# Attention in blocks and a feed-forward layer on one core: a new order for the first tile, its transpositions in single sum banks, and spare products

## The chip, the core and the metric

The kernel runs on one core of a Trainium2 chip. The core has TensorE (PE in the rows: matrix products into the sum banks, with PEld for its weight loads), VectorE (DVE), ScalarE (ACT), GpSimd (POOL) and SyncE (SP), which issues the transfers. The engines run side by side, each through its own instructions in order, and wait for each other by semaphores. Sums of TensorE stand in eight banks of 128 x 512 numbers. The metric is the device time of one execution in microseconds (us).

## The reference

For 8 batches, 8 heads, 576 positions and 64 features per head the kernel computes attention inside blocks of 64 positions, and then a layer with a residual over the 512 features of all heads:

```
scores = (q @ k.T) / sqrt(64)              # per block of 64 x 64
attn   = exp(scores - max); attn /= (sum(attn) + 1e-9)
x      = attn @ v                          # heads side by side: (8, 576, 512)
xn     = (x - mean) / sqrt(var + 1e-6) * g
out    = x + relu(xn @ w1) @ w2            # w1: 512 x 2048, w2: 2048 x 512
```

All arrays are 32-bit; the weights reach the kernel as 64-bit words and are turned into 32-bit numbers on the chip.

## The kernel before

The 4608 positions are cut into 18 pairs of 256 and 9 tiles of two pairs. For a pair, `attention` goes through thirteen steps: load q and k (L186), scores (L206), the maximum and the load of v (L213, L216), subtraction and exponential (L219, L223), the transposition of the probabilities `pt` (in the first two tiles by TensorE, L231, with copies by ScalarE), the products with v (L271; in the first tile with the row sums beside them, L275), x (L286), statistics (L304), `xg` (x less its mean, times g, L309), and the transposition of `xg` into `xt` (L321). `xt` is kept as a rounded high part `xth` (L324) and a low part `xtl`, which TensorE makes by adding the high part times minus one (`minus`) to the same sum bank (L328, L331).

`ffn` then takes 16 hidden blocks f: an up (12 products, L369), the high part `hh` and low part `hl` of its positive part (L377 on ScalarE, L378 on VectorE), and a down (six products for a pair, L389) into the pair's two sum banks `y`. In the first tile blocks 0 to 5 are done for each pair by itself (256 columns), the other ten for both (512 columns).

The weights come in 17 units (two half units, then 15 whole ones of 1.05 MB): fetched by SP (L104), absolute value on ScalarE (L112), rounding on VectorE (three operations, L119 to L123), the sign (L129), the high part by ScalarE (L133), and the low part `wl`, for the first four units by TensorE through the sum banks of pair 1 (L144 to L146), for the others by VectorE (L148). Three buffers hold fetched units, one the absolute values.

The sum banks: one buffer `s` of two banks, through which scores, `pt`, attention outputs and `xt` of every pair of the first two tiles pass in turn; two banks `h`; four banks `y`, two for each pair of a tile.

What stands where is written by hand: `START` is a string of letters, and each letter plays one step of one stream: a, b the attention of the first tile's pairs, A, B of the second tile's, E of the third's first pair; w the weights; u and 1, v and 2, y and 3 the products and the rectified parts of the first tile. `STEADY` and `LAST` order the other tiles. Each engine gets its instructions in that order, the SP queue too.

Of the kernel before, what the change touches and what calls it, by code (L numbers as in the profile page):

```python
# [13 lines left out]
AF = mybir.ActivationFunctionType  # L14
# [3 lines left out]
P = 128  # L18
# [5 lines left out]
NPAIR = T // PAIR  # L24
NTILE = NPAIR // 2
# [6 lines left out]

START = "aawwwwaawwwwwwawbwawwawbwbabwwaawaaawwbwwuA1wbbu1uwuwuAuB1Awubu1u1Awbwuu1bbbbuwvwAvw22AwAAvvvvB2EwA2wvv2vABvy2w3yBvwAww3vAyAwwywwyw3yA3BwyBwByByByBw3wB3wyByBww3yyBwwyEw3wywyy33yy3"
STEADY = "ABu1Au1AuAu1AuAu1AuABuAu1AEu1AuAu1AuAu1AuAu1BuBu1BuBu1BuBu1BuBEuBBu1BBu1BuBBu1Buu1uu1"
LAST = "u1u1uu1uu1uu1uu1uu1uu1uu1uu1uu1uu1uu1uu1uu1uu1u1"

SINGLE = 6

BY_PE = 4

ROOM = (3, 11)

# [9 lines left out]
def chunk_attention_ffn(ctx: ExitStack, tc: tile.TileContext, qkv, g, w, out):  # L54
# [15 lines left out]
    ident = const.tile([P, P], F32, name="ident")  # L70
    make_identity(nc, ident)
    minus = const.tile([P, P], F32R, name="minus")
    nc.scalar.activation(minus, ident, AF.Copy, scale=-1.0)
    ones = const.tile([P, 2], F32, name="ones")
    nc.gpsimd.memset(ones, 1.0)
    mhalf = const.tile([P, 2], F32, name="mhalf")
# [74 lines left out]
    def convert_w():  # L151
# [18 lines left out]
        split_w(units - 1)  # L170
        yield

    ys, taken = {}, set()

    def sums(pair):
# [5 lines left out]
    def attention(pair, xt_cols, xs, by_pe, den_by_pe):  # L181
# [10 lines left out]
        def banks():  # L192
            return ps_a.tile([P, 2, DM], F32, name="s")

        def rows(bank):
            return bank.rearrange("p (a d) -> p a d", d=D)

        s2 = banks()
        s = [rows(s2[:, h2, :]) for h2 in range(2)]
# [26 lines left out]

        pt_sb = work.tile([P, groups, 2, D], F32, name="pt_sb", tag="work")
        if by_pe:
            pt = banks().rearrange("p j (a t) -> p j a t", a=HP)
            for a in range(groups):  # L230
                nc.tensor.transpose(out=pt[:, a // HP, a % HP, :], in_=p_sb[:, a, :, :], identity=ident)  # L231
            for j in range(2):
                nc.scalar.copy(
                    pt_sb[:, j * HP : (j + 1) * HP], pt[:, j].rearrange("p a (c t) -> p a c t", c=2)
                )
            yield
        else:
            for h2 in range(2):
                for j in range(2):
                    for c in range(2):  # L240
                        for i in range(2):
                            nc.vector.transpose(  # L242
                                out=pt_sb[quad(2 * h2 + j), :, c, quad(i)], in_=p_sb[quad(2 * c + i), :, h2, quad(j)]
                            )
                    yield
# [67 lines left out]

        xth, xtl = xt_cols()
        if by_pe:
            xt = banks()
            for j in range(2):
                js = slice(j * P, (j + 1) * P)
                for k in range(NK):
                    ks = slice(k * P, (k + 1) * P)  # L320
                    nc.tensor.matmul(  # L321
                        xt[:, j, ks], lhsT=xg[:, j, ks], rhs=ident, is_transpose=True, start=k == 0, stop=k == NK - 1
                    )
                nc.scalar.copy(xth[:, :, js], xt[:, j, :].rearrange("p (k t) -> p k t", k=NK))  # L324
                yield
            for j in range(2):
                js = slice(j * P, (j + 1) * P)
                nc.tensor.matmul(  # L328
                    xt[:, j, :], lhsT=minus, rhs=xth[:, :, js], start=False, stop=True, skip_group_check=True
                )  # L330
                nc.scalar.copy(xtl[:, :, js], xt[:, j, :].rearrange("p (k t) -> p k t", k=NK))  # L331
                if j == 0:
                    yield
        else:
            xt = work.tile([P, 2 * NK, P], F32, name="xt", tag="work")
            xg = xg.rearrange("p j (k t) -> p (j k) t", k=NK)
            for j in range(4):
                for i in range(4):
                    nc.vector.transpose(out=xt[quad(j), :, quad(i)], in_=xg[quad(i), :, quad(j)])  # L339
                yield  # L340
            for j in range(2):
                js = slice(j * P, (j + 1) * P)
                xt_j = xt[:, j * NK : (j + 1) * NK, :]
                nc.scalar.copy(xth[:, :, js], xt_j)  # L344
                nc.gpsimd.tensor_tensor(out=xtl[:, :, js], in0=xt_j, in1=xth[:, :, js].bitcast(F32), op=ALU.subtract)  # L345
# [7 lines left out]
    def ffn(pairs, xt, xs, f0, f1, room=()):  # L353

        nt = len(pairs) * PAIR
        slots = DM // nt
        hs, held = {}, []
        tail = pairs[-1] == NPAIR - 1

        def up(f):  # L360
            assert 2 * f in converted and all(pair in xs for pair in pairs)
            h = ps_h.tile([P, nt], F32, name="h")
            xth, xtl = xt()
            m = 0
            for k in range(NK):
                ks = slice(k * P, (k + 1) * P)
                wh, wl = (x[:, ks] for x in weights(f))
                for wx, x in ((wh, xth), (wh, xtl), (wl, xth)):
                    nc.tensor.matmul(h, lhsT=wx, rhs=x[:, k, :], start=m == 0, stop=m == 3 * NK - 1)  # L369
                    m += 1  # L370
            hs[f] = h

        def split(f):
            if slots == 1 or not held:
                held[:] = [hp_.tile([P, slots, nt], F32R, name=f"h{i}") for i in "hl"]
            h, (hh, hl) = hs[f], (x[:, f % slots, :] for x in held)
            nc.scalar.activation(hh, h, AF.Relu)  # L377
            nc.vector.scalar_tensor_tensor(  # L378
                out=hl, in0=h, scalar=0.0, in1=hh.bitcast(F32), op0=ALU.max, op1=ALU.subtract
            )  # L380
            hs[f] = hh, hl

        def down(f, j):
            assert 2 * f + 1 in converted
            taken.add(pairs[j // 2])
            hh, hl = (x[:, j * P : (j + 1) * P] for x in hs[f])
            wh, wl = (x[:, DM:] for x in weights(f))
            for m, (hx, wx) in enumerate(((hh, wh), (hh, wl), (hl, wh))):
                nc.tensor.matmul(  # L389
                    sums(pairs[j // 2])[j % 2], lhsT=hx, rhs=wx,  # L390
                    start=f == 0 and m == 0, stop=f == NF - 1 and m == 2,
                )

        def finish(j):
            pair, jj = pairs[j // 2], j % 2
            x, rstd = xs[pair]
            nc.vector.scalar_tensor_tensor(  # L397
                out=x[:, jj, :], in0=sums(pair)[jj], scalar=rstd[:, jj : jj + 1], in1=x[:, jj, :],
                op0=ALU.mult, op1=ALU.add,
            )  # L400
            row = pair * PAIR + jj * P
            nc.sync.dma_start(out[row : row + P, :], x[:, jj, :])

        count = 2 * len(pairs)
        done = []

        def products():
            ups = iter(range(f0, f1))
            for f in range(f0, f1):
                for _ in range((f not in room) + (f == f0 or f - 1 in room or tail and f == NF - 3)):  # L410
                    i = next(ups, None)
                    if i is not None:
                        up(i)
                        yield
                if tail and f >= NF - 2:
                    continue
                for j in range(count):
                    down(f, j)
                done.append(f)
                yield  # L420
            if tail:
                for j in range(count):
                    for f in range(NF - 2, NF):
                        down(f, j)
                done.append(NF - 1)
                yield

        def rectified():
            for f in range(f0, f1):
                assert f < f0 + 2 or f - 2 in done  # L430
                split(f)
                yield
            if f1 == NF:
                assert NF - 1 in done
                for j in range(count):
                    finish(j)
                yield

        return products(), rectified()
# [3 lines left out]
    def play(order, streams):  # L443
        for c in order:
            next(streams[c])
# [3 lines left out]
    class Tokens:  # L449
# [18 lines left out]
    now = {  # L468
        "a": tiles[0].attention(0, True, True), "b": tiles[0].attention(1, True, True),
        "A": tiles[1].attention(0, True), "B": tiles[1].attention(1, True),  # L470
        "E": tiles[2].attention(0), "w": convert_w(),
    }
    now.update(zip("u1", tiles[0].ffn(0, 1, 0, SINGLE)))
    now.update(zip("v2", tiles[0].ffn(1, 1, 0, SINGLE)))
    now.update(zip("y3", tiles[0].ffn(0, 2, SINGLE, NF)))
    with tc.manual_schedule():
        play(START, now)
        for t in range(1, NTILE):
            now.update(zip("u1", tiles[t].ffn(0, 2, room=ROOM if t + 1 < NTILE else ())))
            if t + 1 < NTILE:  # L480
                now.update(A=now.pop("E"), B=tiles[t + 1].attention(1))
            now["E"] = tiles[t + 2].attention(0) if t + 2 < NTILE else iter("  ")
            play(STEADY if t + 1 < NTILE else LAST, now)
# [33 lines left out]
```

## Time and profile before

| | |
|---|---|
| median of 3 runs | 882.14 us (881.94 to 883.23) |
| profiled execution | 884.8 us, span 883.0 us |
| TensorE busy | 856.3 us, 97% of the span |
| VectorE, ScalarE, GpSimd busy | 538.3, 173.6, 50.6 us |
| loads and stores | 55.67 MB moved, mean 63 GB/s |

A busy time is the time in which an engine has at least one instruction running; start and duration of an instruction are those of the hardware profiler. The chain that ended last leads from the end back to what released each step. The granted clock of TensorE (PEclk) is 1.00 at 2.4 GHz and 0.50 at 1.2 GHz.

### The profile page before, as it was taken

The page shows a single profiled execution, that of the slowest core. Times are in us where ns is not written, and L with a number is a line of the kernel's source. Part 1 is how long each engine was busy: PE and PEld are TensorE (multiplying, and loading weights), DVE is VectorE, ACT ScalarE, POOL GpSimd, SP SyncE. Part 2 cuts the span into 40 slices and gives each one's busy share as a digit, 9 for nine tenths or more (in the row PEclk, how much of TensorE's full clock was granted, in tenths as well). Part 3 has the DMA queues.
Part 4 walks back from the last instruction along what each step waited for, and adds up shares of the span by engine and source line. Part 5 has one row for each costly group of instructions (what it writes and reads, how often), then busy time and mean ns, then how long its engine had stood idle before and what let it go on. Part 6 is the DMA issues. An engine that isn't in the chain of part 4 may idle for free.

```text
span 883.0 us, 13918 instructions
## 1 busy us (share of the span) xinstructions
PE 856.3 (97%) x6050; PEld 706.4 (80%) x6050; DVE 538.3 (61%) x963; ACT 173.6 (20%) x262; POOL 50.6 (6%) x54
## 2 busy tenths in 40 slices
PE   4699999999999999999999999999999999999998
PEld 3378788888888888888888888888888888888886
DVE  5988885657575666567656766666566657661112
ACT  4543541111111211021112120212120111111110
POOL 0000000010100110010101010101010101010000
PEclk9799999999999999999999999999999999999999
DMA  7554241310032003200320032003200210010001
GB/s 298 206 201 168 95 144 49 104 39 1 1 120 72 1 1 119 73 1 1 119 73 1 1 120 73 1 1 120 73 1 1 79 66 0 1 48 1 1 1 48
DMA packets 18205, 55.67 MB, mean 63 GB/s; under 512 B 2017, under 2 KB 2017, under 8 KB 16225
## 3 DMA queue, kind: packets, MB, share of 16 engines
q1 hardware_dynamic: 18000, 54.53, 17.4%
q8 instruction: 47, 0.77, 0.4%
q10 hardware_dynamic: 144, 0.26, 0.1%
q14 instruction: 14, 0.11, 0.0%
HBM read 45.35 MB, written 9.44 MB: 62 GB/s over the span
## 4 chain that ended last, share of the span: by engine, by line
PE 97%; DVE 1%; issue 1%; ACT 1%; DMA 1%; SPq 0%
PE y L389 45%; PE h L369 45%; PE s L206 2%; PE h L271 2%; PE s L231 1%; DMA k_t<-qkv 1%; PE y L144 1%; PE s L271 1%; PE s L321 0%; PE s L328 0%; ACT xtl L331 0%; ACT xth L324 0%; PE y L275 0%; DVE raw L123 0%; DVE top L213 0%
## 5 line engine op out<-in xcount | busy, mean ns | idle before, releaser
L369 PE MATMUL h<-xth,wp 128*128 128x512 f32 (+1 forms) x1200 | 379.3, 382 | 0.0
L389 PE MATMUL y<-wp,hh 128*128 128x512 f32 x1152 | 358.1, 392 | 0.0
L378 DVE SCALAR_TENSOR_TENSOR hl<-h,hh 128x512 fp32r<-128x512 f32 (+1 forms) x150 | 100.4, 669 | 285.5 <-ACT hh L377 285.0
L369 PEld LDWEIGHTS h<-xth,wp 128*128 128x128 f32 x1200 | 224.0, 189 | 43.5
L389 PEld LDWEIGHTS y<-wp,hh 128*128 128x128 f32 x1152 | 214.8, 188 | 44.7 <-ACT hh L377 0.2
L369 PE MATMUL h<-xtl,wp 128*128 128x512 f32 (+1 forms) x600 | 228.9, 381 | 0.0
L389 PE MATMUL y<-wp,hl 128*128 128x512 f32 x576 | 224.9, 390 | 0.0
L377 ACT ACTIVATE hh<-h 128x512 fp32r<-128x512 f32 (+1 forms) x150 | 87.1, 580 | 575.8 <-PE h L369 556.3
L369 PEld LDWEIGHTS h<-xtl,wp 128*128 128x128 f32 x600 | 113.3, 189 | 21.9
L389 PEld LDWEIGHTS y<-wp,hl 128*128 128x128 f32 x576 | 108.4, 188 | 23.2 <-DVE hl L378 0.4
L339 DVE STREAM_TRANSPOSE xt<-xg 32x256 f32<-32x256 f32 x224 | 97.7, 436 | 3.7
L242 DVE STREAM_TRANSPOSE pt_sb<-p_sb 32x256 f32<-32x256 f32 x224 | 97.6, 436 | 3.1
L345 POOL TENSOR_TENSOR xtl<-xt,xth 128x512 fp32r<-128x512 f32 x28 | 35.6, 1292 | 609.4 <-ACT xth L344 609.4
L397 DVE SCALAR_TENSOR_TENSOR x<-y,rstd,x 128x512 f32<-128x512 f32 x36 | 25.3, 750 | 18.4 <-PE y L389 18.4
L206 PE MATMUL s<-k_t,q_t 64*64 64x64 f32 x1152 | 21.3, 224 | 7.9 <-DMA k_t<-qkv 6.8
L213 DVE TENSOR_REDUCE top<-s 128x16 f32<-128x1024 f32 x18 | 21.9, 1216 | 9.6 <-PE s L206 9.6
L223 ACT ACTIVATE p_sb<-p_sb 128x1024 f32<-128x1024 f32 x18 | 19.1, 1061 | 44.0 <-DVE p_sb L219 44.0
L206 PEld LDWEIGHTS s<-k_t,q_t 64*64 64x64 f32 x1152 | 19.4, 140 | 9.4 <-issue 9.2
L294 DVE TENSOR_TENSOR x<-h,rden 128x512 f32<-128x512 f32 x28 | 18.0, 686 | 12.1 <-PE h L271 12.1
L309 DVE SCALAR_TENSOR_TENSOR xg<-x,mv,g_sb 128x512 f32<-128x512 f32 x36 | 25.3, 743 | 0.0
L304 DVE BATCH_NORM_STATS2 stats<-x 128x6 f32<-128x512 f32 x36 | 24.3, 675 | 0.3
L112 ACT ACTIVATE wf<-raw 128x1024 f32<-128x1024 f32 (+1 forms) x17 | 18.7, 1100 | 21.7 <-DMA raw<-w 13.1
(47 smaller groups left out, 306.5 us busy)
## 6 DMA issues: line engine op xcount, KB each, us to landing
raw<-w SPq DMA_DIRECT2D x15, 1024.0 KB, 4.8
q_t<-qkv SPq DMA_DIRECT2D x18, 512.0 KB, 4.6
k_t<-qkv SPq DMA_DIRECT2D x18, 512.0 KB, 5.5
v_t<-qkv SPq DMA_DIRECT2D x36, 256.0 KB, 4.9
out<-x SPq DMA_DIRECT2D x36, 256.0 KB, 2.1
raw<-w SPq DMA_DIRECT2D x2, 512.0 KB, 6.7
g_sb<-g ACTq DMA_DIRECT2D x1, 256.0 KB, 4.8
```

The source lines that it names most:

```text
L206: nc.tensor.matmul(s[h2][c * D : (c + 1) * D, j * HP + a, :], lhsT=q_t[r, a, cs], rhs=k_t[r, a, cs], start=True, stop=True,)
L242: nc.vector.transpose(out=pt_sb[quad(2 * h2 + j), :, c, quad(i)], in_=p_sb[quad(2 * c + i), :, h2, quad(j)])
L271: nc.tensor.matmul(rows(o[h2])[cs, ja, :], lhsT=lhsT, rhs=v_t[j][r, a, c, :], start=True, stop=True)
L304: nc.vector.bn_stats(out=stats, in_=x[:, j, :])
L309: nc.vector.scalar_tensor_tensor(out=xg[:, j, :], in0=x[:, j, :], scalar=mv[:, j, 0:1], in1=g_sb, op0=ALU.subtract, op1=ALU.mult)
L339: nc.vector.transpose(out=xt[quad(j), :, quad(i)], in_=xg[quad(i), :, quad(j)])
L345: nc.gpsimd.tensor_tensor(out=xtl[:, :, js], in0=xt_j, in1=xth[:, :, js].bitcast(F32), op=ALU.subtract)
L369: nc.tensor.matmul(h, lhsT=wx, rhs=x[:, k, :], start=m == 0, stop=m == 3 * NK - 1)
L377: nc.scalar.activation(hh, h, AF.Relu)
L378: nc.vector.scalar_tensor_tensor(out=hl, in0=h, scalar=0.0, in1=hh.bitcast(F32), op0=ALU.max, op1=ALU.subtract)
L389: nc.tensor.matmul(sums(pairs[j // 2])[j % 2], lhsT=hx, rhs=wx, start=f == 0 and m == 0, stop=f == NF - 1 and m == 2,)
L397: nc.vector.scalar_tensor_tensor(out=x[:, jj, :], in0=sums(pair)[jj], scalar=rstd[:, jj : jj + 1], in1=x[:, jj, :], op0=ALU.mult, op1=ALU.add,
```

## The change

Three things change. First, in the first tile `pt` and `xt` of a pair no longer take the two-bank buffer `s` but the pair's own two sum banks (`halves`), each half a bank for itself; `taken` only marks them in use while the order is recorded. Second, a stream `keep_warm`, letter k, issues eight products of `minus` with itself into the first sum bank; nobody reads them. The new order plays it four times: once ahead of everything, and three times in a row between the low part of the second half unit and the scores of pair 1. Third, `START` is new. `minus` is now made at the head of the recorded order.

```diff
-START = "aawwwwaawwwwwwawbwawwawbwbabwwaawaaawwbwwuA1wbbu1uwuwuAuB1Awubu1u1Awbwuu1bbbbuwvwAvw22AwAAvvvvB2EwA2wvv2vABvy2w3yBvwAww3vAyAwwywwyw3yA3BwyBwByByByBw3wB3wyByBww3yyBwwyEw3wywyy33yy3"
+START = "wkwwawwwwwwbwwawwkkkbaawawwbbwaabawaaawAbwbaauubbAw11bbAbbuwAuuwBAuAAv1uw1vA2uwuBw2w1wvwvv2uAw1uvAyuwvw2v3wyBywBvw23EvwwwAy2wAwywy3AAwwwyv3BwwyBBByByBwB3vB3Bywwyyw3wBywww3ywy3wyy3yy3E"
...
+WARM = 8
...
-    nc.scalar.activation(minus, ident, AF.Copy, scale=-1.0)
...
+    def keep_warm():
+        while True:
+            assert 0 not in taken
+            for i in range(WARM):
+                nc.tensor.matmul(sums(0)[0][:, :P], lhsT=minus, rhs=minus, start=True, stop=True)
+            yield
...
+        def halves():
+            if den_by_pe:
+                assert pair not in taken
+                return sums(pair)
+            both = banks()
+            return [both[:, j, :] for j in range(2)]
...
-            pt = banks().rearrange("p j (a t) -> p j a t", a=HP)
+            pt = halves()
             for a in range(groups):
-                nc.tensor.transpose(out=pt[:, a // HP, a % HP, :], in_=p_sb[:, a, :, :], identity=ident)
+                cs = slice(a % HP * P, (a % HP + 1) * P)
+                nc.tensor.transpose(out=pt[a // HP][:, cs], in_=p_sb[:, a, :, :], identity=ident)
...
-            xt = banks()
+            xt = halves()
+            if den_by_pe:
+                taken.add(pair)
...
-        "E": tiles[2].attention(0), "w": convert_w(),
+        "E": tiles[2].attention(0), "w": convert_w(), "k": keep_warm(),
...
     with tc.manual_schedule():
+        nc.scalar.activation(minus, ident, AF.Copy, scale=-1.0)
         play(START, now)
```

In the SP queue q and k of pair 0 stood first (L186), and then four fetches of weights (L104). Now the two half units and unit 2 are fetched first, then q and k of pair 0, unit 3, q and k of pair 1, unit 4 and v of pair 0.

VectorE, at the start of the program. `top` and `p_sb` belong to the attention, `wf` and `raw` to the weights. Before:

```order
L213 TENSOR_REDUCE top<-s 128x16
L219 TENSOR_TENSOR p_sb<-s,top 128x2x8x64
L119 TENSOR_SCALAR wf<-wf 128x512
L120 TENSOR_SCALAR wf<-wf 128x512
L123 SCALAR_TENSOR_TENSOR raw<-raw,wf 128x512
L129 SCALAR_TENSOR_TENSOR raw<-raw 128x512
```

and now, from the second half unit on (the first stands ahead of it in the same four rows):

```order
L120 TENSOR_SCALAR wf<-wf 128x512
L121 TENSOR_SCALAR wf<-wf 128x512
L124 SCALAR_TENSOR_TENSOR raw<-raw,wf 128x512
L130 SCALAR_TENSOR_TENSOR raw<-raw 128x512
L120 TENSOR_SCALAR wf<-wf 128x1024
L121 TENSOR_SCALAR wf<-wf 128x1024
L124 SCALAR_TENSOR_TENSOR raw<-raw,wf 128x1024
L130 SCALAR_TENSOR_TENSOR raw<-raw 128x1024
L230 TENSOR_REDUCE top<-s 128x16
L236 TENSOR_TENSOR p_sb<-s,top 128x2x8x64
```

Both half units and the first whole unit stand ahead of the first maximum, where none stood before.

VectorE, from the row sums of pair 0 (`den`) to its `xg`. Before:

```order
L281 TENSOR_SCALAR den<-y 128x8 x2
L282 RECIPROCAL rden<-den 128x16
L286 TENSOR_TENSOR x<-s,rden 128x2x8x64
L129 SCALAR_TENSOR_TENSOR raw<-raw 128x1024
L213 TENSOR_REDUCE top<-s 128x16
L304 BN_STATS stats<-x 128x6
L305 BN_AGGR mv<-stats 128x2
...
L219 TENSOR_TENSOR p_sb<-s,top 128x2x8x64
L119 TENSOR_SCALAR wf<-wf 128x1024
L120 TENSOR_SCALAR wf<-wf 128x1024
L123 SCALAR_TENSOR_TENSOR raw<-raw,wf 128x1024
L309 SCALAR_TENSOR_TENSOR xg<-x,mv,g_sb 128x512 x2
```

and now:

```order
L299 TENSOR_SCALAR den<-y 128x8 x2
L300 RECIPROCAL rden<-den 128x16
L304 TENSOR_TENSOR x<-s,rden 128x2x8x64
L322 BN_STATS stats<-x 128x6
L323 BN_AGGR mv<-stats 128x2
...
L327 SCALAR_TENSOR_TENSOR xg<-x,mv,g_sb 128x512 x2
L130 SCALAR_TENSOR_TENSOR raw<-raw 128x1024
```

The sign of a unit, the maximum and subtraction of pair 1 and a unit's rounding no longer stand between x and `xg`; the pair 1 steps have moved ahead of the row sums.

TensorE, at the start of the program, `y<-raw,ident` and `y<-wp,minus` being the low part of a half unit. Before:

```order
L206 MATMUL s<-k_t,q_t 64x64 x32
L144 MATMUL y<-raw,ident 128x512
L145 MATMUL y<-wp,minus 128x512
L231 MATMUL s<-ident,p_sb 128x128 x8
L144 MATMUL y<-raw,ident 128x512
```

and now:

```order
L179 MATMUL y<-minus 128x128 x8
L145 MATMUL y<-raw,ident 128x512
L146 MATMUL y<-wp,minus 128x512
L223 MATMUL s<-k_t,q_t 64x64 x32
L145 MATMUL y<-raw,ident 128x512
L146 MATMUL y<-wp,minus 128x512
L179 MATMUL y<-minus 128x128 x24
L223 MATMUL s<-k_t,q_t 64x64 x32
L249 MATMUL y<-ident,p_sb 128x128 x8
```

The spare products stand first and ahead of the second scores, the scores of both pairs ahead of the first transpositions, and these write `y` instead of `s`.

## Rows read from the trace of the kernel before

**Rows 1.** Stretches: length; busy (count) of PE, PEld, DVE, ACT, POOL; PEclk, DMA, GB/s

```profile
0.00:42.00 42.00, 21.78 (x301) 14.06 (x301) 30.47 (x41) 21.26 (x28) 1.98 (x9) 0.88 0.67 244
70.00:860.00 790.00, 789.33 (x5357) 654.61 (x5357) 478.73 (x881) 136.28 (x212) 47.04 (x44) 1.00 0.14 49
```

**Rows 2.** Waits of TensorE, 0 to 70 us: line, releaser, us, times, longest

```profile
PE s L321 <- DVE xg L309: 4.3, 1, 4.3
```

**Rows 3.** Timeline of VectorE: start, duration, line, operation

```profile
8.84 1.23 DVE L213 TENSOR_REDUCE top<-s 128x16 f32<-128x1024 f32 x1 [8.84 <-PE s L206]
...
11.24 0.42 DVE L119 TENSOR_SCALAR wf<-wf 128x512 f32<-128x512 f32 x1
...
13.62 0.43 DVE L119 TENSOR_SCALAR wf<-wf 128x512 f32<-128x512 f32 x1
...
23.05 0.23 DVE L281 TENSOR_SCALAR den<-y 128x8 f32<-128x8 f32 x2
...
24.75 1.22 DVE L129 SCALAR_TENSOR_TENSOR raw<-raw 128x1024 uint32<-128x1024 uint32 x1
...
27.47 0.68 DVE L304 BATCH_NORM_STATS2 stats<-x 128x6 f32<-128x512 f32 x1
...
29.09 1.19 DVE L219 TENSOR_TENSOR p_sb<-s,top 128x1024 f32<-128x1024 f32 x1
...
30.19 0.68 DVE L119 TENSOR_SCALAR wf<-wf 128x1024 f32<-128x1024 f32 x1
...
32.78 1.41 DVE L309 SCALAR_TENSOR_TENSOR xg<-x,mv,g_sb 128x512 f32<-128x512 f32 x2
...
34.11 1.22 DVE L129 SCALAR_TENSOR_TENSOR raw<-raw 128x1024 uint32<-128x1024 uint32 x1
...
81.32 0.39 DVE L378 SCALAR_TENSOR_TENSOR hl<-h,hh 128x256 fp32r<-128x256 f32 x1
```

**Rows 4.** Stretches around the fall and the rise of the granted clock (PEclk)

```profile
32.00:33.00 1.00, 0.00 (x0) 0.00 (x0) 1.00 (x2) 0.10 (x1) 0.00 (x0) 0.61 1.12 475
...
45.00:46.00 1.00, 1.00 (x52) 1.00 (x49) 0.75 (x2) 1.00 (x2) 0.00 (x0) 0.57 0.86 344
```

**Rows 5.** Chain that ended last, 0 to 72 us: start, us, what

```profile
6.80 1.99 PE s L206 x64
...
40.27 1.97 PE s L231 x8
...
42.24 2.56 PE h L369 x12
...
53.16 1.09 PE s L206 x64
...
57.26 1.43 PE h L369 x12
...
58.69 1.39 PE y L389 x6
...
67.30 2.56 PE y L389 x6
...
71.30 0.77 PE s L231 x7
```

**Rows 6.** Stretches from the start, for the data moved (last column GB/s)

```profile
0.00:5.35 5.35, 0.00 (x0) 0.00 (x0) 0.00 (x0) 1.28 (x1) 0.77 (x8) 1.00 0.66 216
0.00:6.67 6.67, 0.00 (x0) 0.00 (x0) 0.00 (x0) 1.28 (x1) 0.77 (x8) 1.00 0.73 254
0.00:11.60 11.60, 1.99 (x64) 1.83 (x64) 2.72 (x3) 2.39 (x4) 0.77 (x8) 1.00 0.85 324
```

**Rows 7.** Timeline of ScalarE

```profile
7.95 0.67 ACT L112 ACTIVATE wf<-raw 128x512 f32<-128x512 f32 x1 [5.50 <-DMA raw<-w]
...
11.36 1.06 ACT L223 ACTIVATE p_sb<-p_sb 128x1024 f32<-128x1024 f32 x1 [2.54 <-DVE p_sb L219]
```

**Rows 8.** Waits of VectorE, 47.3 to 141.4 us

```profile
DVE hl L378 <- ACT hh L377: 9.5, 9, 1.9
```

More of the change, by code (lines that the diff above doesn't have):

```diff
@@ L228, in attention @@
         if by_pe:
-            pt = banks().rearrange("p j (a t) -> p j a t", a=HP)
+            pt = halves()
             for a in range(groups):
-                nc.tensor.transpose(out=pt[:, a // HP, a % HP, :], in_=p_sb[:, a, :, :], identity=ident)
+                cs = slice(a % HP * P, (a % HP + 1) * P)
+                nc.tensor.transpose(out=pt[a // HP][:, cs], in_=p_sb[:, a, :, :], identity=ident)
             for j in range(2):
                 nc.scalar.copy(
-                    pt_sb[:, j * HP : (j + 1) * HP], pt[:, j].rearrange("p a (c t) -> p a c t", c=2)
+                    pt_sb[:, j * HP : (j + 1) * HP], pt[j].rearrange("p (a c t) -> p a c t", a=HP, c=2)
                 )
@@ L321, in attention @@
                     nc.tensor.matmul(
-                        xt[:, j, ks], lhsT=xg[:, j, ks], rhs=ident, is_transpose=True, start=k == 0, stop=k == NK - 1
+                        xt[j][:, ks], lhsT=xg[:, j, ks], rhs=ident, is_transpose=True, start=k == 0, stop=k == NK - 1
                     )
-                nc.scalar.copy(xth[:, :, js], xt[:, j, :].rearrange("p (k t) -> p k t", k=NK))
+                nc.scalar.copy(xth[:, :, js], xt[j].rearrange("p (k t) -> p k t", k=NK))
                 yield
@@ L328, in attention @@
                 nc.tensor.matmul(
-                    xt[:, j, :], lhsT=minus, rhs=xth[:, :, js], start=False, stop=True, skip_group_check=True
+                    xt[j], lhsT=minus, rhs=xth[:, :, js], start=False, stop=True, skip_group_check=True
                 )
-                nc.scalar.copy(xtl[:, :, js], xt[:, j, :].rearrange("p (k t) -> p k t", k=NK))
+                nc.scalar.copy(xtl[:, :, js], xt[j].rearrange("p (k t) -> p k t", k=NK))
                 if j == 0:
                     yield
+            if den_by_pe:
+                taken.remove(pair)
         else:
@@ L357, in ffn @@
         hs, held = {}, []
-        tail = pairs[-1] == NPAIR - 1
+        tail = pairs[-1] == 2 * NTILE - 1
         def up(f):
```

## The prediction

> **What bounds the kernel now.** I read the busy times of long stretches first. From 70 to 860 us TensorE is busy for 789.33 of 790 us at full clock, so nothing there can be gained or moved; from 0 to 42 us it is busy for only 21.78 [rows 1]. The change rewrites the order of the first tile alone, so the whole question lies in the first 70 us.
>
> Second, the waits of TensorE: 4.3 us for `xg`, a VectorE result, is the longest after the first keys, for which it stands until 6.80 us [rows 2, 5]. Third, therefore, VectorE's own timeline: it stands idle until the scores arrive at 8.84 us and then runs almost without a gap, turn by turn on weights and attention [rows 3]. Up to about 40 us TensorE waits for VectorE and, behind it, for the order of the loads.
>
> Fourth, the clock. It falls in the slice 32 to 33 us (0.61), inside TensorE's 4.3 us wait for `xg`, and rises in 45 to 46 us (0.57) [rows 2, 4]. At the low level 12 up products take 2.56 us instead of 1.43, and 6 down products 2.56 instead of 1.39 [rows 5]. The first 64 score products took 1.99 us against 1.09 later [rows 5], so the start ran at the low level too, although the slices there print 1.00.
>
> **The landmark for the sum.** At 69.86 us (67.30 + 2.56) the kernel before has finished all six hidden blocks of pair 0; from there it runs full [rows 5]. I look for the time at which the new order has done a known part of the same work and count the difference in warm durations. The landmark of the new order is the end of pair 2's eight probability transpositions (p of `A`). By then it has done all that the old one has done at 69.86, except three ups (blocks 3, 4, 5) and four downs (2 to 5), and it has done eight transpositions more, which the old one starts only at 71.30 us. The difference is 3 × 1.43 + 4 × 1.39 − 0.87 = 8.98 us (0.87 from 0.77 for the seven transpositions that the row shows) [rows 5].
>
> **When the first weights land.** In the new SP queue both half units of weights (0.52 MB each) and unit 2 (1.05 MB) stand ahead of the first queries and keys. The table g (0.26 MB) goes on another queue beside them. Before, the first keys ended 1.31 MB of queued data and were there just ahead of the scores at 6.80, about 6.67 us, when 254 × 6.67 = 1.69 MB had moved [rows 5, 6]: data land 0.38 MB behind their place. The first half unit now ends 0.78 MB, so it lands when 1.16 MB have moved, at 5.35 us (216 × 5.35) [rows 6]. The keys now end 3.41 MB and land at 3.79 MB, 11.6 us (324 × 11.6 = 3.76) [rows 6]: 4.9 us later than before. ScalarE's absolute value takes 0.67 us [rows 7]; VectorE starts at about 6.0 instead of 8.84. Bounds: with no lag at all 0.9 us earlier, with twice the lag 0.9 us later; I keep the middle, which is the measured lag.
>
> **VectorE's chain to the landmark.** Its queue is in order, so I add what stands in it, start to start [rows 3]: a half unit of weights 2.38; a full unit 2.59 to round (30.19 to 32.78) and 1.22 for the sign; maximum and subtraction 2.40 (8.84 to 11.24); sums and x 1.70 (23.05 to 24.75); statistics 1.62; xg 1.33 (32.78 to 34.11); a low part `hl` of 256 columns 0.39.
> - 6.0 + two half units 4.76 = 10.8; unit 2 waits for ScalarE until 11.2 (it has one buffer for the absolute values).
> - Unit 2: 15.0. Scores a can start at 11.6 and at the low clock end at 13.6, so there is 1.4 us of room. Maximum and subtraction a: 17.4. Unit 3: 21.2.
> - Maximum and subtraction b: 23.6. Rounding unit 4: 26.2. Sums and x of a: 27.9. Statistics: 29.5. xg a: 30.9. It was 34.1 before.
> - Sign 4 and rounding 5: 34.7. Sums and x of b 36.4, statistics 38.0, xg b 39.3.
> - Low weights of unit 4, as a sign 1.22: 40.5. Two `hl`: 41.3. Maximum A 1.2, sign 5 1.22, subtraction A 1.2: 44.9.
> - The exponential 1.06 [rows 7] and the transpositions 0.87: 46.9 us.
>
> TensorE's own work lies beside this: first ups after the residues of `xt` a at about 34.7, two ups 37.6, scores A 38.7, `xt` b and its residues 40.8, a down, an up and a down to 45.2. It waits under 1 us for the exponential. So 46.9 holds.
>
> The sum: 69.86 − 46.9 = 22.96, less 8.98 = 14.0 us.
>
> **What the other parts cost.** The 32 spare products: eight stand in the first wait. The other 24 stand between the second half unit's low part and scores b. Half of the 256-column step at the low clock (0.21 in 2.56 / 12) makes 0.11 each, 2.6 us, from 16.1 to 18.7; as dear as the full step it would be 5.1, to 21.2. Scores b need 1.99 at most and VectorE asks for them at 21.2: nothing in the first case, 2.0 us in the second. I take nothing, as the columns are halved. The new scores wait for keys issued after scores a (13.6), which lands inside the same window.
>
> The single banks: before, scores, transpositions, outputs and `xt` of both pairs pass through one two-bank buffer `s`, so that b's transpositions start only at 40.27 us, behind the residues of a [rows 5]. Now `pt` and `xt` of pairs 0 and 1 lie in the pairs' own sum banks, and b's transpositions need only its exponential, which is due about 26 us. Their own worth is between nothing and this whole shift of some 14 us, since the new order would wait in `s` without them; it is already in the chain above and is not added. The moved `minus` is one 128-column cast on ScalarE, ahead of first weights that land at 5.35 us, when ScalarE has only a table load before it: nothing, and at most the 0.67 us of a half unit's absolute value.
>
> What is late next: from 44.9 VectorE has some 28 us of work without a break, and each up from block 6 waits for its unit of weights. By adding the same steps, unit 7's low part is ready at about 65.5 and TensorE asks for it at 66.0; unit 8 at 73.0 and 72.9. There is no margin, so I take 1 us off. After 80 us TensorE's blocks are 512 wide and VectorE gets ahead. Forecast: 13 us. The profiled execution took 884.8 us, 2.7 above the median 882.14; the same difference stays, and the time is **869.0 us**, own range 866 to 872.
>
> **The rivals.**
> 1. *The clock is not kept.* What speaks for it: before, it stayed low until the slice 45 to 46 us though TensorE was working from 40.27 on [rows 4, 5], and in the new order transpositions and single products with ScalarE turns between them stand from 26 to 33 us. Against: the spare products and three dense stretches. Price: the first two ups, PV of b, scores A and a first down at the low level: 2 × 1.13 + 0.9 + 1.17 = 4.3, less about 1.3 us in which TensorE waits anyway: 3 us, 872. Another way is that the change doesn't do what it says, and the spares do nothing for the clock: then only the stage before 26 us is slower, which VectorE hides, and the time stays 869.
>
>  The Trainium skill, "TensorE: Matmul & The Clock Gate", Part 4 (PE-mode transpose), says that transpositions on this engine do not count as work for the full clock. The trace agrees as far as it goes: the clock was still low for the ups from 42.24 us, right behind the eight transpositions at 40.27 [rows 5]. By that rule the time would be this rival's, 872; by the row alone the spares and the two low parts of unit 3 carry the clock over.
>
> 2. *VectorE becomes the bound.* My chain lets it run without a gap up to 75 us. From 47.3 to 141.4 us of the old order it waited 9.5 us for the high parts `hh`, a tenth of the time [rows 8]. If it loses a tenth of its 28 us in the new order too, TensorE loses 2.8 us more: 872. Against: `hh` comes from ScalarE, which has time, and the new order puts `hl` a whole up later than its product. Both together 875.
>
> 3. *Slower.* One mechanism: TensorE stays at the low level right through the first ups, because no stretch of it is dense enough. Then each us of work from 34.7 on costs half a us too much; from 61 us on (13 / 0.5 = 26 us later) it has eaten the whole gain, and at 70 us the time is 887. The low level of the ups at 42.24 and of the downs at 67.30, both behind stretches with small waits [rows 5], speaks for it; that it rose again each time (0.57 in 45 to 46 us; 1.43 for the ups at 57.26) [rows 4, 5] speaks against.
>
> 4. *More than forecast.* Data land without the lag, unit 7 and 8 are in time, and the one wait of 0.67 us left after 70 us goes [rows 1]: 0.9 + 1 + 0.7 more, 866; below 864 only if the early chain is much shorter than added.
>
> **How the numbers follow.** Forecast 0.58, clock 0.14, VectorE 0.12, both 0.04, more 0.08, slower or nothing 0.04. The range 864 to 875 leaves out the slower rival and half of the last two. A measurement of this kernel tells 0.2% (1.8 us) from no change. All cases but the third lie below 880: faster 0.95, same 0.02, slower 0.03.
>
> **What would show it.** Right: VectorE's first rounding at about 6 us, scores a at about 11.6, xg a ending near 31, first ups near 35, the transpositions of A ending near 47 at full clock, and from there one unbroken TensorE to the end. Wrong: a granted clock of 0.5 after 35 us (rival 1), waits of up products for low weights between 60 and 80 us (rival 2), or scores b starting after 21 us, which would make the spares dear.

## The result, and the profile after

The median after is 874.76 us (873.57 to 876.58, 4 runs) against 882.11 us (881.94 to 883.23) for the kernel before, run beside it: a ratio of 0.9916 [0.9895, 0.9937], 7.35 us or 0.8% less. The forecast was 13.1 us. The direction was right, but only 0.56 of the forecast gain is there: the time lies outside the forecast's own range of 866 to 872 us, and only just inside the wider one of 864 to 875 that leaves room for the rivals. The profiled execution after took 875.53 us (span 873.7); before it took 884.8 (883.0), so the two profiles differ by 9.3 us, 2 more than the medians.

First the stretches of the kernel after. Columns: stretch; length, then busy us (count) of PE, PEld, DVE, ACT, POOL; granted clock, DMA share, GB/s.

```profile
0.00:42.00 42.00, 30.99 (x488) 23.59 (x488) 32.64 (x49) 22.62 (x31) 1.48 (x9) 0.96 0.70 257
20.00:21.00 1.00, 0.56 (x21) 0.60 (x25) 0.97 (x2) 0.00 (x0) 0.00 (x0) 0.68 0.99 410
...
23.00:24.00 1.00, 1.00 (x8) 1.00 (x7) 0.70 (x1) 0.50 (x1) 0.00 (x0) 0.62 0.27 102
60.00:80.00 20.00, 20.00 (x171) 17.46 (x170) 18.87 (x26) 8.04 (x12) 0.00 (x0) 1.00 0.40 144
80.00:140.00 60.00, 58.65 (x333) 48.25 (x332) 47.84 (x61) 26.31 (x35) 3.28 (x2) 1.00 0.32 119
140.00:860.00 720.00, 720.00 (x4830) 596.33 (x4829) 418.17 (x802) 105.97 (x169) 44.65 (x42) 1.00 0.13 42
```

In the first 42 us TensorE is busy 30.99 us where it was 21.78 [rows 1]. The clock falls once, for 3.4 us between 20 and 24 us, instead of from 32 to 46 [rows 4]; after that it is full. From 60 to 80 us TensorE has no gap. Between 80 and 140 us 1.35 us are missing, and then nothing up to 860 us.

The waits of TensorE, 0 to 70 us: who waited for whom, us in all, times, longest. The 4.3 us for `xg` [rows 2] is gone; the longest now is for the first weights, and a wait for keys, once for each pair, stands in the list.

```profile
PE y L145 <- DVE raw L130: 4.0, 1, 4.0
...
PE s L223 <- DMA k_t<-qkv: 1.9, 2, 1.0
```

VectorE's timeline (start, duration, line, operation; in brackets the idle time before it and what ended it), to be read beside [rows 3]:

```profile
6.36 0.43 DVE L120 TENSOR_SCALAR wf<-wf 128x512 f32<-128x512 f32 x1 [6.36 <-ACT wf L113]
...
22.48 1.23 DVE L230 TENSOR_REDUCE top<-s 128x16 f32<-128x1024 f32 x1 [0.69 <-PE s L223]
24.20 1.22 DVE L236 TENSOR_TENSOR p_sb<-s,top 128x1024 f32<-128x1024 f32 x1 [0.50 <-PE y L249]
25.79 0.69 DVE L120 TENSOR_SCALAR wf<-wf 128x1024 f32<-128x1024 f32 x1 [0.36 <-ACT wf L113]
...
31.91 1.41 DVE L327 SCALAR_TENSOR_TENSOR xg<-x,mv,g_sb 128x512 f32<-128x512 f32 x2
```

The chain that ended last, 2 to 52 us (start, us, what; DMA is a load from issue to landing, SPq the issuing by SyncE), beside [rows 5]:

```profile
2.93 9.06 DMA k_t<-qkv
...
12.12 2.02 PE s L223 x64
14.16 0.33 SPq L195
...
14.59 5.60 DMA k_t<-qkv
...
20.43 1.99 PE s L223 x64
22.42 1.70 PE y L249 x8
...
26.22 6.32 DMA raw<-w
...
49.58 0.87 PE s L249 x8
```

Here the loss can be read. Scores a end at 14.14; only then are q and k of pair 1 asked for, because they take the same buffer. The keys land at 20.19 (14.59 + 5.60). Scores b start at 20.43, with the clock fallen, and take 1.99 us; VectorE waits 0.69 us for them, then 0.50 us for pair 0's transpositions, then 0.36 us for ScalarE, which stood behind the copies of `pt`. So `xg` a ends near 33.3 (31.91 + 1.41) instead of 30.9. One wait more stands behind it: unit 5's weights go into the buffer of unit 2, could be asked for only at 26.22, when unit 2's low part was done, and landed at 32.54 (26.22 + 6.32). ScalarE waited for them and began the copies of `xt` a 2.7 us after `xg` a began (with both buffers in the experiments below it is 1.5). The landmark, the end of the transpositions of `A`, comes at 49.58 + 0.87 = 50.45 us; 46.9 was forecast. The chain of the kernel before has this for the first load of keys:

```profile
1.16 5.50 DMA k_t<-qkv
```

After the landmark, from 70 us to the end, TensorE has two waits more:

```profile
PE s L348 <- ACT xth L344: 0.7, 1, 0.7
PE s L348 <- ACT xtl L351: 0.7, 1, 0.7
```

The sum with the measured landmark: 69.86 − 50.45 − 8.98 = 10.4. The two waits are 1.4 us where before had one of 0.7 after 70 us, and the stretch behind the last product is 0.2 us longer (3.94 against 3.76): 0.9 less is 9.5, and the two profiles differ by 9.3. The way of counting holds; the landmark and the reference were off. The experiments below bear the counting out: after and six variants of it that leave the work behind the landmark alone have landmarks from 47.4 to 51.4 us, and their profiled times stand 824.9 to 825.1 us above them.

### The profile page after: what moved, and what is told of

The parts are those of the page before. It is cut to its first block, busy times and chain, and to the rows that moved or that the text cites. A ratio compares the mean times of both kernels' runs of the same rounds, so it can differ in the third digit from the quotient of the medians.

```text
span 873.7 us, 13992 instructions
## 1 busy us (share of the span) xinstructions
PE 857.1 (98%) x6082; PEld 708.7 (81%) x6082; DVE 538.2 (62%) x963; ACT 173.5 (20%) x262; POOL 51.0 (6%) x54
## 4 chain that ended last, share of the span: by engine, by line
PE 96%; DMA 2%; ACT 1%; issue 0%; SPq 0%; DVE 0%; ACTq 0%
PE y L411 45%; PE h L391 45%; PE s L223 2%; PE h L289 2%; DMA k_t<-qkv 2%; DMA raw<-w 1%; PE s L289 0%; PE s L341 0%; PE s L249 0%; PE y L249 0%; ACT wf L113 0%; ACT wp L147 0%; ACT xtl L351 0%; PE s L348 0%; PE y L348 0%
## 5 line engine op out<-in xcount | busy, mean ns | idle before, releaser
L419 DVE SCALAR_TENSOR_TENSOR x<-y,rstd,x 128x512 f32<-128x512 f32 x36 | 25.3, 750 | 18.7 <-PE y L411 18.7
L236 DVE TENSOR_TENSOR p_sb<-s,top 128x1024 f32<-128x1024 f32 x18 | 21.9, 1219 | 0.8 <-PE y L249 0.5
```

Of the source, the lines that this page charges most:

```text
L419: nc.vector.scalar_tensor_tensor(out=x[:, jj, :], in0=sums(pair)[jj], scalar=rstd[:, jj : jj + 1], in1=x[:, jj, :], op0=ALU.mult, op1=ALU.add,
```

## The experiments

My theory after the result: late keys of pair 1 cost the largest part, and the profiled execution before was no typical one. The rivals: the spares do harm, the low clock is the cost by itself, `work`'s two buffers are, or the weights ahead of the first keys are. Each ratio is against runs of the kernel before on the same chip, whose medians were 882.5 to 883.0 us.

### Spares taken out

```diff
-START = "wkwwawwwwwwbwwawwkkkbaaw...
+START = "wwwawwwwwwbwwawwbaaw...
```

> The changed kernel without its 32 spare products. My theory: the spares cost and give nothing, because the second scores wait for the keys of pair 1 (20.2 us) and not for the spares (done at 19.4), and the clock falls at 20.3 us in spite of them; 874.8 us, within 1 us. Rival: they carry the clock through a part of the stage; without them the products from 20 to 34 us run longer at the low level, 1.5 to 3 us slower, 876.3 to 877.8. Second rival: they hold scores b back; 0.5 to 1 us faster.

Measured 873.82 us (873.57 to 874.27), ratio 0.9899 [0.9881, 0.9916]: not slower than with them. By the medians it is 0.9 us faster, which the theory (within 1 us) and the second rival (0.5 to 1 us) both allow; the runs of the two kernels overlap. Stretches without spares (columns as above):

```profile
18.00:19.00 1.00, 0.05 (x4) 0.08 (x5) 0.97 (x2) 0.81 (x1) 0.00 (x0) 0.91 0.99 356
...
22.00:23.00 1.00, 1.00 (x7) 0.74 (x6) 0.87 (x2) 0.95 (x2) 0.00 (x0) 0.89 0.25 88
```

The chain without spares:

```profile
14.39 4.32 DMA k_t<-qkv
...
18.95 1.99 PE s L223 x64
```

The clock falls without the spares as it does with them, and about as long (3.4 us). The keys land 1.5 us earlier here (18.71 against 20.19), with one profile of each; why they do is open. The landmark follows them: 48.50 against 50.45 us. The spares bring nothing that these runs can tell. That they hold scores b back, as the second rival says, isn't what the profile of after shows: they were done at 19.42, ahead of the keys.

### The old order with the new banks

`START` is that of the kernel before, all else that of the kernel after:

```diff
-START = "wkwwawwwwwwbwwawwkkkbaaw...
+START = "aawwwwaawwwwwwawbwawwawb...
```

> The order of before (its START, no spares) with pt and xt of pairs 0 and 1 in single sum banks. Theory A: the banks matter by themselves, since half 1 of xt no longer waits for the copy of half 0 out of the common buffer; the waits of 0.7 to 0.8 us at 35 to 40 and at 62 to 67 us (seven, about 5 us) go in part, and the fall of the clock at 66 us with them: 877 to 880 us. Theory B (the prediction's): the chain goes by VectorE, the banks only make the new order possible; 881 to 882.5 us.

Measured 878.69 us (877.75 to 879.34), ratio 0.9951 [0.9939, 0.9964]: the banks alone are worth 4.0 us. The waits of TensorE, 24 to 72 us, in a further profile of the kernel before (the first of the two that are told of below):

```profile
PE s L321 <- ACT xth L324: 1.9, 2, 1.2
PE s L328 <- ACT xtl L331: 1.4, 2, 0.7
PE s L328 <- ACT xth L324: 1.3, 2, 0.7
...
PE s L231 <- ACT xtl L331: 0.7, 1, 0.7
```

The same waits with the old order and the new banks:

```profile
PE y L341 <- DVE xg L327: 4.7, 1, 4.7
...
PE y L348 <- ACT xth L344: 0.7, 1, 0.7
```

Before, `xt` was one tile over two banks: TensorE's half 1 waited until ScalarE had copied half 0, and pair 1's transpositions until both halves were copied. These waits are 1.9 + 1.4 + 1.3 + 0.7 = 5.3 us; with a bank for each half 0.7 us is left. The wait for `xg` stays (4.3 us before, [rows 2]), as it should, and a new one of 0.6 us for `hl` takes a little back.

### Keys of pair 1, probabilities of pair 1, and both, in buffers of their own

The late steps each wait for a buffer. They get space that the weights of late units need only later:

```diff
-        q_t = load.tile([P, HP, PAIR], F32, name="q_t")
-        k_t = load.tile([P, HP, PAIR], F32, name="k_t")
+        if pair == 1:
+            qk = const.tile([P, 2, HP, PAIR], F32, name="qk_own", tag="w12")
+            q_t, k_t = qk[:, 0], qk[:, 1]
+        else:
...
-        p_sb = work.tile([P, groups, 2, D], F32, name="p_sb", tag="work")
+        if pair == 1:
+            p_sb = const.tile([P, 2 * groups, 2, D], F32, name="p_own", tag="w13")[:, :groups]
+        else:
...
```

The first edit alone:

> The changed kernel, only q and k of pair 1 in a buffer of their own. My theory: the late keys are the whole loss of this stage; scores b start at about 19.2 us at full clock, the clock does not fall at 20 us, and subtraction b finds the transpositions of a done; like both buffers together, 872.5 to 873.2 us. Rival: the buffer of the probabilities has its share; 873.5 to 874.3.

The second alone:

> The changed kernel, only the probabilities of pair 1 in a buffer of their own. My theory: scores b still start at about 20.3 us behind their keys, and rounding 4 still waits for ScalarE, which copies the transpositions of a first; no gain, 874.2 to 875.2 us. Rival: subtraction b's wait for the transpositions (0.5 us) is what the chain loses; 0.5 to 1 us faster, 873.8 to 874.2.

Both, and both without spares:

> The changed kernel, q and k of pair 1 and its probabilities each in a buffer of their own, so that the keys are loaded without waiting for scores a and subtraction b does not wait for the transpositions of a. My theory: scores b then start behind the spares at 19.4 instead of 20.43, and subtraction b starts at about 22.7 instead of 24.2; the chain through rounding 4 comes 1 to 1.5 us earlier and so does everything to the end: 873.3 to 873.8 us. Rival: a later wait (weights of unit 5 landing at 32.5, ScalarE) binds anyway: 874.8.

> The same as the one with both buffers of their own, without the spare products. My theory: scores b start right behind the low part of the second half unit (about 17.9, when subtraction a releases the buffer), the copies of pt a end near 22.7, rounding 4 starts near 24.2 instead of 25.8: 872.8 to 873.5 us. Rival: without the spares the clock stays low through the stage, 1.5 to 3 us slower than with them: 875 or more.

| own buffer of pair 1 | median us (range) | ratio | scores b start | landmark |
|---|---|---|---|---|
| none (after) | 874.76 (873.57 to 876.58) | 0.9916 [0.9895, 0.9937] | 20.43 | 50.45 |
| q and k | 872.68 (872.40 to 872.99) | 0.9886 [0.9869, 0.9903] | 19.17 | 47.5 |
| probabilities | 875.09 (873.78 to 875.54) | 0.9910 [0.9894, 0.9926] | 20.82 | 49.6 |
| both | 872.73 (872.63 to 873.02) | 0.9885 [0.9871, 0.9900] | 19.11 | 47.78 |
| both, no spares | 873.14 (872.24 to 874.02) | 0.9889 [0.9874, 0.9905] | 17.86 | 47.4 |

The keys alone give the whole 2.1 us, the probabilities nothing. With both buffers the time came 0.6 us below its forecast. The chain with q and k in their own buffer:

```profile
16.39 2.85 PE y L179 x24
19.24 1.09 PE s L227 x64
20.33 1.02 PE y L253 x8
```

With both buffers, the timeline of VectorE, and behind it that of TensorE:

```profile
29.97 1.38 DVE L334 SCALAR_TENSOR_TENSOR xg<-x,mv,g_sb 128x512 f32<-128x512 f32 x2
...
43.87 1.22 DVE L243 TENSOR_TENSOR p_sb<-s,top 128x1024 f32<-128x1024 f32 x1
```

```profile
19.11 1.16 PE L227 MATMUL s<-qk_own 64*64 64x64 f32 x64
...
35.69 0.39 PE L398 MATMUL h<-xtl,wp 128*128 128x256 f32 x1 [0.81 <-ACT xtl L358]
...
46.74 1.04 PE L256 MATMUL s<-ident,p_sb 128*128 128x128 f32 x8
```

Scores b follow the work before them without a wait and at full clock: 1.09 us, not 1.99. With both buffers `xg` a ends near 31.3 (30.9 forecast), subtraction A near 45.1 (44.9) and the landmark is 46.74 + 1.04 = 47.78 (46.9 forecast). So VectorE's chain was added up rightly but for the arrival of pair 1's keys. The 0.9 us that are left are TensorE's: the exponential of A is done near 46.2, but the downs ahead of the transpositions end at 46.9 and not at 45.2, as the first up waits 0.81 us for the low part of `xt` a. Without spares the clock did not fall either in the profiled execution.

In the kernel with the probabilities alone TensorE waited 1.7 us ahead of scores b, longer than the 1.0 us of after, and yet the clock stayed full there. Its wait, and the stretch of scores b:

```profile
PE s L223 <- DVE raw L124: 1.7, 1, 1.7
...
21.00:22.00 1.00, 1.00 (x65) 0.93 (x61) 0.85 (x1) 0.00 (x0) 0.00 (x0) 1.00 1.00 397
```

The profile names VectorE as the releaser, but scores b read nothing of `raw`. The keys were asked for at 14.66 and took 5.9 us, so they landed at about 20.56, 0.26 us ahead of scores b; in after it was 0.25. This execution also answers the rival that the low clock is the cost by itself: the clock was full, and the landmark still came 1.8 us later than with both buffers. Late keys cost without the fall; what the fall adds to them was not measured apart.

### Spares in the old order

The old order with the new banks, and 32 spares in TensorE's longest wait:

```diff
-START = "...bwbabwwaawaaawwbwwuA1...
+START = "...bwbabwwakkkkawaaawwbwwuA1...
```

> The order of before with single sum banks, and 32 spare products in the wait of 4.7 us for xg of pair 0 (29 to 33.5 us). Theory A: spare products hold the clock; then it does not fall near 31 us, the products from 33.5 to 41 us run at full level, and the time is 2 to 3 us below the 878.7 of the same kernel without them. Theory B (from the kernel without spares): they do not count enough; the clock falls all the same and the time is 878.7 within 1 us.

Measured 878.23 us (877.39 to 878.35), ratio 0.9946 [0.9933, 0.9959]; without the spares it was 878.69 (0.9951 [0.9939, 0.9964]). TensorE's timeline:

```profile
28.27 3.68 PE L179 MATMUL y<-minus 128*128 128x128 f32 x32
33.05 1.62 PE L341 MATMUL y<-ident,xg 128*128 128x128 f32 x8 [1.10 <-DVE xg L327]
```

Stretches of the same kernel, around the fall and the rise of the clock:

```profile
33.00:34.00 1.00, 0.95 (x6) 0.71 (x7) 1.00 (x2) 1.00 (x3) 0.00 (x0) 0.96 0.00 0
...
40.00:41.00 1.00, 1.00 (x7) 1.00 (x7) 0.96 (x2) 1.00 (x1) 0.00 (x0) 0.62 0.48 188
```

And without the spares:

```profile
31.00:32.00 1.00, 0.00 (x0) 0.00 (x0) 0.97 (x2) 0.08 (x1) 0.00 (x0) 0.51 1.00 418
```

The spares fill 3.68 us of the long wait and only 1.10 us stays idle; the clock falls all the same, 2 us after the last spare, and is low until about 40.8 us. In these two profiles the fall comes 2.9 us later with the spares and its low stretch is some 3.4 us shorter (6.8 against 10.2). The later start alone says little, since the first fall came at 32.2 and at 34.2 in two executions of the kernel before. But the shorter stretch stands in the other executions too: the mean granted clock was 0.996 three times, 0.998 and 1.000 with spares, 0.994 four times and 0.996 twice without. So spares did shorten the fall, and in one execution there was next to none. That one took 877.39 us, 1.3 below the median without spares: even a clock kept brought less in that run than the 2 to 3 us of theory A.

### First keys ahead of the weights

```diff
-START = "wkwwaww...
+START = "awkwwww...
```

> The changed kernel with q and k of pair 0 loaded ahead of the weights again, nothing else moved. My theory: VectorE's first rounding starts near 8 us instead of 6.3 and all of its chain 1.5 to 2 us later, but the keys of pair 1 are asked for at 8.8 us and are no longer late, which gives 2 us back: 874 to 876 us. Rival: the weights ahead are the core of the gain, 876.3 to 878. Second rival: the loads are hidden anyway and only the keys count, 872.5 to 873.5.

Measured 875.99 us (875.65 to 876.53), ratio 0.9923 [0.9911, 0.9936]: 1.2 us above after by the medians, inside the spread of after's own runs. TensorE's timeline:

```profile
10.99 2.04 PE L145 MATMUL y<-raw,ident 128*128 128x512 f32 x2 [6.20 <-DVE raw L130]
...
13.39 1.86 PE L223 MATMUL s<-k_t,q_t 64*64 64x64 f32 x64
...
22.09 1.98 PE L223 MATMUL s<-k_t,q_t 64*64 64x64 f32 x64 [2.88 <-DMA k_t<-qkv]
```

The early keys bring nothing, because scores a stand behind the first half unit's low part in TensorE's queue. They start at 13.39, later than in after (12.12); pair 1's keys are asked for later, and scores b wait 2.88 us for them. The time lies in the theory's range by luck, as the keys of pair 1 were not on time. Putting the weights ahead is worth about 1.2 us by the medians, which these runs can't tell from nothing.

### The kernel before, profiled twice more

The kernel is unchanged.

> The kernel before once more, for its trace: its runs lie near 882.1 or near 884.4 us, and the profiled one (884.8) in the upper group. My theory: the two groups differ by the second fall of the clock at 66 us (3.5 us at the low level, about 2 us dear); a run near 882 has no such fall, a run near 884.5 has one. Rival: they differ at the start (landing of the first loads, 0 to 20 us) and both fall at 66 us.

> The same once more, so that the two groups may both be seen: near 882 without the second fall of the clock, or near 884.5 with it.

They took 882.62 and 882.92 us; a third execution beside them took 885.22. One stretch of the first of the two:

```profile
66.00:67.00 1.00, 1.00 (x5) 0.82 (x6) 1.00 (x2) 0.65 (x2) 1.00 (x1) 1.00 0.00 0
```

Its chain there:

```profile
52.46 1.09 PE s L206 x64
...
66.32 1.38 PE y L389 x6
67.70 1.44 PE h L369 x12
```

The six downs that took 2.56 us from 67.30 [rows 5] take 1.38 us from 66.32: there is no second fall of the clock, and the state of 69.86 us is reached at 67.70 (67.92 in the second). Not all of these 2.16 us are the second fall: at scores A the execution behind the forecast was already 0.70 us later (53.16 [rows 5] against 52.46), most of it lost between 42 and 47 us, where its first fall ended at 45.9 and not at 44.4. The second fall makes the other 1.5 us, less than the 2 of my theory. All runs of the kernel before lie at 881.8 to 883.2 or 884.2 to 885.4; the execution behind the forecast lies with the upper ones. One profile from up there and two from below show the second fall and its absence. Of the other runs there is no trace, but their mean granted clock fits: 0.990 or 0.992 in the upper group, 0.994 in the lower but for one run (882.30 us, 0.992).

### A version that beats both

The keys of pair 1 in their own buffer, and three moves in the order: the last two steps of pair 0 (the residues of its `xt`) ahead of two of pair 1, and a residue step of pair 2 and one of pair 3 behind the y that follows it, so that the last two waits get cover. With and without spares:

```diff
-START = "...awaaawAbwbaauubb...wAwywy3AAwwwyv3B...wB3vB3Byww...
+START = "...awaaawAaabwbuubb...wAwywy3AwwwyAv3B...wB3v3ByBww...
```

> The kernel with q and k of pair 1 in a buffer of their own, and three steps moved in START: the residues of xt a ahead of the products of b with v (so that the first up does not wait 0.8 us for them), and one residue step each of pairs 2 and 3 behind the next down (their waits of 0.7 us near 92 and 110 us). My theory: TensorE is the bound from 50 us on, so each wait removed is worth itself: 1.4 to 2.0 us below the 872.7 without the moves, 870.7 to 871.3. Rival: VectorE has no margin between 45 and 80 us and gives the first one back: 871.8 to 872.3.

> The same without the 32 spare products. My theory: the spares are worth nothing here either, the same time within 0.6 us. Rival: where the wait ahead of scores b is gone they keep the clock for the stage behind it; 1 to 2 us slower without them.

With spares 872.18 us (872.06 to 875.13), ratio 0.9884 [0.9863, 0.9905]; without 871.56 (871.22 to 871.90), ratio 0.9870 [0.9852, 0.9888]. The stretch of 80 to 140 us without spares:

```profile
80.00:140.00 60.00, 60.00 (x398) 49.33 (x397) 48.49 (x61) 24.76 (x33) 2.37 (x2) 1.00 0.33 120
```

The longest new waits of TensorE up to 70 us, with spares:

```profile
PE h L395 <- issue: 1.8, 1, 1.8
PE s L293 <- ACT wp L147: 1.4, 1, 1.4
```

The two waits after the landmark are gone. The steps moved ahead gave part of it back: with spares two waits of 1.8 and 1.4 us stand in the early stage, where the kernel with the keys alone has 0.8 and 0.6. So the forecast of 870.7 to 871.3 was missed with spares; the rival's number came, but that VectorE is the reason isn't shown. Against the kernel with the keys alone (0.9886) the moves with spares bring nothing that can be told. Without spares the median is the lowest of all kernels, 11.4 us below before (883.00 beside it).

## Why the prediction was partly right

The forecast was 13.1 us and 7.35 came. The landmark (3.55 us late) and the reference (2.16 us) make 5.7 of the 5.8 us that are missing. That the time still lies within 864 to 875 is in part luck: that width was there for a low clock and for VectorE as the bound, not for late keys or a false reference. Term by term:

- **"Data land 0.38 MB behind their place", weights first.** Right: VectorE started at 6.36 (6.0 forecast), the first keys were there at 12.0 (11.6), scores a took 2.0 us at the low level as forecast.
- **"The new scores wait for keys issued after scores a (13.6), which lands inside the same window."** This is the step that failed. The keys were asked for at 14.16 and 14.59, took 5.60 us beside two other loads (unit 4 and v, issued at 16.46 and 16.83) and landed at 20.19, behind the spares and not under them. I had priced the transfer at nothing, though the chain of the kernel before has 5.50 us for such a load; from the issue at 14.59 that gives 20.09. Scores b came 1 us late and met a clock that had just fallen, and the wait for the buffer of `p_sb`, the one for ScalarE and the late weights of unit 5 followed. The landmark came 3.55 us late in the profile; the own buffer for q and k gives back 2.1 us in the medians, with the landmark at 47.5.
- **"The profiled execution took 884.8 us, 2.7 above the median; the same difference stays."** Failed too. The difference arose in the stage that the change rewrites: 69.86 against 67.70, of which a second fall of the clock made 1.5 us and a longer first one most of the rest. Against a more typical execution the sum is 67.70 − 50.45 − 8.98 − 0.9 = 7.4 us, and the medians say 7.35; that it is so close is in part luck, as both profiled executions lie above their medians (882.62 against 882.11, 875.53 against 874.76). I should have asked why the profile lay above the median before I used its end of the first stage as the landmark.
- **"There is no margin, so I take 1 us off."** The size was right by luck, the place was not. No up waited for weights between 60 and 80 us (20.00 of 20); what came off were two waits for `xth` and `xtl` and the tail, 0.9 us.
- **VectorE's chain.** Right once the keys are there: with both own buffers subtraction A ends near 45.1 against 44.9.
- **"a down, an up and a down to 45.2", TensorE's own work.** Too short by 1.7 us: with both own buffers the downs end at 46.9, behind a first up that waited 0.81 us, and they and not the exponential set the landmark of 47.78 against 46.9.
- **The spares.** Counted at nothing, and no more can be told: 873.82 without against 874.76 with, 873.14 against 872.73, 871.56 against 872.18. But the 24 took 3.08 us (16.34 to 19.42), 0.13 each and at full clock, not 0.11 at the low one; the halved columns halved nothing, since a 256-column up product takes 1.43 / 12 = 0.12.
- **The banks.** "Already in the chain", and so not added, was right for the sum, but their worth was left between nothing and 14 us and their way was another. With the old order they bring 4.0 us, because half 1 of `xt` no longer waits for the copy of half 0; the other half of the gain comes with the order. That the new order with the single buffer `s` would stand in its own way was argued and not run.

Of the rivals, the first came in part: the clock fell, but at 20 and not at 26 us, and for 3.4 us. The Trainium skill's rule ("TensorE: Matmul & The Clock Gate", Part 4) that transpositions don't count as work for the clock can't be laid to this fall: it began at 20 to 21 us, before the transpositions at 22.42. With the keys on time eight of them ran at full clock (1.02 us) and nothing fell; no run here has a long stretch of them alone. The VectorE rival and the slower one did not occur.

What stays open: why the keys landed between 18.7 and 20.6 us with nearly the same loads, and why the clock fell after a wait of 1.0 us in one execution and not after 1.7 us in another. The runs of after are spread over 3 us, those with the keys in their own buffer over 0.6. That the fall spreads them is not shown: in after the longer runs have the lower mean clock (0.999 at 873.57 and 874.00 us, 0.998 at 875.53, 0.997 at 876.58), but the one long run of the last kernel with spares (875.13 us) had 0.999.

## What to carry to other kernels

When a step is moved forward, follow its load back to the point at which its buffer comes free, and price the transfer from a row with the same neighbours in the queue; "it lands in the same window" is a number to be worked out. Before a landmark is read from one profile, ask whether that execution stands where the median stands, and if not, which stage makes the difference: if it is the stage of the change, the difference does not stay. A tile over two banks is one thing to wait for; giving each half its bank brought about as much here (4.0 of 7.35 us) as the whole new order.

## What the runs showed of the hardware

- A spare product of 128 columns took 0.13 us (3.08 / 24) where the granted clock was 1.00, as much as one of 256 columns at full clock (0.12); the first eight of the program took 0.25 each (1.97 / 8).
- 32 of them right ahead of a wait of 1.10 us did not keep the clock in the profiled execution: it fell 2 us after the last and stayed low for 6.8 us. In one of five executions there was next to no fall (mean granted clock 1.000).
- At the start the profile prints a clock of 1.00 while 64 scores take 2.0 us, as at 0.50 later (1.99), against 1.09 at full clock.
- The load of one k tile (0.5 MB) took 4.2 to 9.6 us from issue to landing (both in the old order with the new banks), with other loads on their way beside it.
